# Order of the seven products, VectorE subtractions and split order in the second layer's pair stages

## The chip, the cores and the metric

The kernel runs on one core of a Trainium2 chip. The time is in device microseconds of that core, from runs of the whole program; a comparison uses the median of several runs. Before the change the median of three runs is 1150.7 us (1148.37 to 1151.74).

## The reference

Three parts follow one another. Only the third is touched by the change, beside the loads that lead to it.

```python
# 1. retention: 4 x 8 heads, 768 steps of 64 x 64 state
state = gamma * state + k[t] (x) v[t];  y[t] = q[t] @ state / 8
x = y.transpose(0, 2, 1, 3).reshape(3072, 512)
# 2. first layer: w_in 512 x 2048, w_out 2048 x 512
h = x @ w_in;  g = (a0 + a1*h + a2*h^2 + a3*h^3) / (1 + |b0||h| + |b1|h^2 + 1e-6);  x = g @ w_out
# 3. second layer, same sizes
h = x @ w_in;  g = h * clip(h + 3, 0, 6) / 6;  out = g @ w_out
```

All tensors are float32. The kernel multiplies in TensorE's reduced float32 form and keeps the accuracy by splitting each operand into a high and a low part and adding three products: high x high, high x low, low x high.

## The kernel before

The 3072 tokens are six blocks of 512. Retention and the first layer go block by block, then the second layer does blocks 0 and 1 in the plain way, in steps numbered `n` (`N1` = 96 is the first step of the second layer, `N2` = 128 the first behind its plain part). The other four blocks go as two pairs, p = 1 and 2 (`second_layer`, L1069). A pair of blocks is a 2 x 2 block matrix product, done by Strassen and Winograd's scheme with seven products in place of eight. Products are called 1 to 7 by their number `q`.

A pair has two stages. In the first, `unit(p, u, part)` (L890) forms, for each of eight slices u of the hidden dimension, the seven products of the inputs `xs[p, q]` with the weights that `win_load` fetched, in the order 1, 6, 2, 7, 5, 4 and, in the next unit, 3. VectorE joins them, and `gate` leaves the gate values of the four blocks, tiles g11, g12, g21 and g22 (`groom`). `whole_sum` makes the sums S of g21 and g22.

The second stage (L1095 to L1110) multiplies the gates with w_out. Its 14 halves are (q, k): `ORDER` gives the order of the products, k the half of the tokens. In the loop over the halves stand, for half i: the load of the next product's weights (`wout_load`, four tiles wo, on SP's queue, at k = 0), the half's 48 matmuls (`product`, L1002, 128 x 256 each), the evacuation of half i - 1 (`evac`), the split of half i + 2 (`g_split`), and for pair 1 the jobs of `xc_jobs` for pair 2's inputs.

`g_split` (L964) makes the high and low parts, tiles s, of one half in four quarters j. `source` gives what is split: for products 1, 2, 4 and 5 a gate tile or S as it stands; for 6, 7 and 3 VectorE first forms it in place (S - g11, then g11 - g21, then g12 - S). ScalarE copies the high part (L972), VectorE subtracts it (L977, by the helper line L731). In products 6, 7 and 3 the quarter j = 0 goes another way:

```python
if j == 0 and q in (6, 7, 3):
    nc.scalar.activation(lo, f32(hi), AF.Copy, scale=-1.0)              # L974
    nc.gpsimd.dma_start(out=f32(lo), in_=src, accum_op=ALU.add)         # L975, POOL's queue
```

`evac` (L1027) scales the results. Products 1 and 2 add up in bank A, 6 and 7 in bank B, 5 and 3 in bank C, and 4 starts afresh in bank B. For product 1 and 2 ScalarE does it (L1032, L1048); for 6, 3 and 4 VectorE does one operation, for 7 two (L1025). Results go out by `store` (L1019) on SP's queue.

Pair 2's inputs are loaded, combined and split by `xc_jobs(2)` (L1112), which says behind which half of pair 1 each job is emitted: `xc_load` at 5 and 6, `xc_sums` at 8 and 9, and the 14 calls of `xc_split`, three a half, from 9 on. `xc_split` is a ScalarE copy (L829) and a VectorE subtraction. Behind half 12 the first weights of pair 2 are loaded (`win_load`, L843, on SP's queue). For pair 1 the same calls are put into steps by L1304 to L1309.

Buffers of 128 x 1024 are rooms of one pool: `take` hands out the room that was given back first, `give` puts it at the end of the list. Who writes into a room waits for its last reader. Each engine and each queue works its instructions in the order of emission; every wait is a wait of all that stands behind it there.

Weight sums: the scheme needs sums of weight blocks. `prep_at(n, kind, u)` (L792) puts one into the steps: load at n - 1, four VectorE operations at n (`prep_sums`), ScalarE copies at n + 1, two VectorE subtractions at n + 2 (`prep_lo`), stores to DRAM on POOL's queue at n + 2, rooms back at n + 4. `LATE` holds the steps, counted from `N1`, of seven of them; the last three are of w_out (tiles zwo). From step 130 on a step of this list is emitted behind a unit of pair 1.

Of the kernel before, what the change touches and what calls it, by code (L numbers as in the profile page):

```python
# [12 lines left out]
AF = mybir.ActivationFunctionType  # L13
ALU = mybir.AluOpType
# [10 lines left out]
SPARE = ("wi14", "wi15", "wo14", "wo15")  # L25
WARM, WARM_AGAIN = 3, 3
PREP, FAR, AHEAD = 50, 9, 4
KEPT, LATE = 14, (18, 20, 22, 24, 31, 33, 34)
Q_CONST = 1.0 + 1e-6
LN_SCALE = 2.0**16  # L30
G_SCALE = -1.0 / LN_SCALE**2
# [3 lines left out]
def tile_retention_moe_moe2(  # L35
# [13 lines left out]
    nc = tc.nc  # L49
# [632 lines left out]


    PAIRS, FIRST = NBLK // 2, 1
    ORDER = (1, 5, 6, 7, 3, 2, 4)
    LEFT = {1: 0, 2: 1, 4: 3, 5: 4, 6: 5, 7: 6, 3: 7}
    RIGHT = {1: 0, 2: 2, 3: 3, 5: 4, 6: 5, 7: 6, 4: 7}
    smalls, bigs, spare_half, taken = deque(), deque(), ([], []), {}
# [25 lines left out]
    def take_two(name):  # L714
        return take_big(name) if bigs else (take(name + "h"), take(name + "l"))

    def give(*tiles):
        for t in tiles:
            place = taken.pop(id(t))
            if isinstance(place, tuple):  # L720
                smalls.append(place)
            else:
                place[1] -= 1
                if place[1] == 0:
                    bigs.append(place[0])

    def f32(t):
        return t.bitcast(F32)

    def tensor(engine, out, a, b, op):  # L730
        engine.tensor_tensor(out=out, in0=a, in1=b, op=op)  # L731
# [91 lines left out]
    def xc_split(p, c, q):  # L823
        a, b, d, e = (f32(t) for t in xraw[p, c])
        src = {1: a[:, 0:512], 2: b[:, 0:512], 3: b[:, 512:1024], 5: d[:, 0:512], 6: d[:, 512:1024], 7: e[:, 0:512], 4: e[:, 512:1024]}[q]
        if c == 0:
            xs[p, q] = take_two(f"x{p}_{q}")
        hi, lo = (t[:, c * 512 : (c + 1) * 512] for t in xs[p, q])
        nc.scalar.activation(hi, src, AF.Copy)  # L829
        tensor(nc.vector, lo, src, f32(hi), ALU.subtract)  # L830
        if q == 4:
            give(*xraw.pop((p, c)))


# [55 lines left out]
    def unit(p, u, part):  # L890
        nm = f"{p}_{u}"
        if part == 0:
            if u == 0:
                live[p] = ps_at.tile([128, 1024], F32, tag="at", name=f"a{p}")
            now = live[p, u] = {"A": live[p][:, 0:512]}
            mm1(p, u, 1, now["A"], True)
            if u:
                last_two(p, u - 1, 0)
            now["s1"] = g_p.tile([128, 512], F32, tag="gh", name="s1" + nm)
            nc.scalar.activation(now["s1"], now["A"], AF.Copy)  # L900
            now["B"] = ps_h.tile([128, 512], F32, tag="h", name="hB" + nm)
            mm1(p, u, 6, now["B"], True)
            now["U2"] = t2.tile([128, 512], F32, tag="u", name="U2" + nm)
            tensor(nc.vector, now["U2"], now["B"], now["s1"], ALU.add)
        elif part == 1:
            now = live[p, u]
            if u:
                mm1(p, u - 1, 3, live[p, u - 1]["C"], False)
                last_two(p, u - 1, 1)
            mm1(p, u, 2, now["A"], False)  # L910
            gate(p, 11, u, now["A"], relu(now["A"], "11_" + nm))
        else:
            now = live[p, u]
            mm1(p, u, 7, now["B"], False)
            U3 = t2.tile([128, 512], F32, tag="p", name="U3" + nm)
            tensor(nc.vector, U3, now["B"], now.pop("s1"), ALU.add)
            now["C"] = ps_h.tile([128, 512], F32, tag="h", name="hC" + nm)
            mm1(p, u, 5, now["C"], True)
            h22 = g_p.tile([128, 512], F32, tag="gl", name="h22" + nm)
            tensor(nc.vector, h22, now["C"], U3, ALU.add)  # L920
            gate(p, 22, u, h22, relu(h22, "22_" + nm))
            if (p, u) == (FIRST, 0):
                now["D"] = live[p][:, 512:1024]
            else:
                now["D"] = ps_acc.tile([128, 512], F32, tag="acc0", name="hD" + nm)
            mm1(p, u, 4, now["D"], True)
            tensor(nc.vector, U3, now["D"], U3, ALU.add)
            now["h21"] = U3

    sums, splits, wout, halves = {}, {}, {}, [(q, k) for q in ORDER for k in range(2)]

# [30 lines left out]
    def g_split(p, q, k, js=range(4)):  # L964
        if (p, q, k) not in splits:
            splits[p, q, k] = [take(f"s{p}_{q}_{k}_{i}") for i in range(4)]
        rooms = splits[p, q, k]
        for j, src in [(j, source(p, q, k, j)) for j in js]:
            hi, lo = (
                rooms[i + j // 2].rearrange("p (f t) -> p f t", f=4)[:, j % 2 * 2 : j % 2 * 2 + 2, :] for i in (0, 2)  # L970
            )
            nc.scalar.activation(hi, src, AF.Copy)  # L972
            if j == 0 and q in (6, 7, 3):
                nc.scalar.activation(lo, f32(hi), AF.Copy, scale=-1.0)  # L974
                nc.gpsimd.dma_start(out=f32(lo), in_=src, accum_op=ALU.add)  # L975
            else:
                tensor(nc.vector, lo, src, f32(hi), ALU.subtract)  # L977
        if k == 1 and 3 in js:
            dead = {7: (21, 11), 2: (12,), 4: (22,)}.get(q, ())
            give(*(groom.pop((p, x, j)) for x in dead for j in range(4)))  # L980
            if q == 3:
                give(*(sums.pop((p, j)) for j in range(4)))
# [84 lines left out]
            smalls.extend([(raw_p, "raw")] * 2)  # L1067

    def second_layer():  # L1069
        for p in range(FIRST, PAIRS):  # L1070
            for u in range(NU):
                last = u == NU - 1
                if (p, u) != (FIRST, 0):
                    unit(p, u, 0)
                    unit(p, u, 1)
                    if u > 1 and u % 2 == 0:
                        whole_sum(p, u // 2 - 1)
                    if not last:
                        win_load(p, u + 1)
                    unit(p, u, 2)  # L1080
                    if p == FIRST:
                        for parts in (begin, middle, before, after):
                            for fn, *args in parts.get(N2 + LAG + u - 1, ()):
                                fn(*args)
                if last:
                    give(*(t for q in (1, 6, 2, 7, 5, 4) for t in xs.pop((p, q))))
                    wout_load(p, ORDER[0])
                    g_split(p, 1, 0, range(3))
            g_split(p, 1, 0, (3,))
            mm1(p, NU - 1, 3, live[p, NU - 1]["C"], False)  # L1090
            last_two(p, NU - 1, 0)
            last_two(p, NU - 1, 1)
            whole_sum(p, NU // 2 - 1)
            give(*xs.pop((p, 3)))
            jobs_x = xc_jobs(p + 1) if p + 1 < PAIRS else {}  # L1095
            g_split(p, *halves[1])
            for i, (q, k) in enumerate(halves):
                at = ORDER.index(q)
                if k == 0 and at + 1 < len(ORDER):
                    wout_load(p, ORDER[at + 1])  # L1100
                product(p, q, k)
                if i:
                    evac(p, *halves[i - 1])
                if i + 2 < len(halves):
                    g_split(p, *halves[i + 2])
                for fn, *args in jobs_x.get(i, ()):
                    fn(*args)
                if p + 1 < PAIRS and (q, k) == (ORDER[-1], 0):
                    win_load(p + 1, 0)
            evac(p, *halves[-1])  # L1110

    def xc_jobs(p):  # L1112
        js = {5: [(xc_load, p, 0)], 6: [(xc_load, p, 1)]}
        splits_due = []
        for c in range(2):
            js[8 + c] = [(xc_sums, p, c, 0, nc.vector), (xc_sums, p, c, 1, nc.vector)]
            splits_due += [(xc_split, p, c, q) for q in (1, 2, 3, 5, 6, 7, 4)]
        for i, job in enumerate(splits_due):
            js.setdefault(9 + i // 3, []).append(job)
        return js  # L1120

    segs = [(0, 0, 0, CUT1), (0, 1, 0, FT), (0, 0, CUT1, FT)] + [(0, b, 0, FT) for b in range(2, NBLK)]
# [121 lines left out]
    def put(where, n, fn, *args):  # L1244
        where.setdefault(n, []).append((fn, *args))
# [41 lines left out]
    for key in (VIA, NBLK, NBLK + 1):  # L1287
        n = at_of[0, key, 0] if key < NBLK else at_of[1, key - NBLK, 0]
        for c in range(KD):

            if key == VIA:
                at, lag = n - 9 + c + 2 * (c > 1), 1
            elif key == NBLK + 1:
                at, lag = n - 5 + c, 1
            else:
                at, lag = n - 12 + 2 * c, 2
# [7 lines left out]
    for c, at in enumerate((23, 26)):  # L1304
        put(begin, N1 + at, xc_load, FIRST, c)
        put(before, N1 + at + 1, xc_sums, FIRST, c, 0, nc.vector)
        put(before, N1 + at + 2, xc_sums, FIRST, c, 1, nc.vector)
        for i, q in enumerate((1, 2, 3, 5, 6, 7, 4)):
            put(before, N1 + at + 2 + i // 2, xc_split, FIRST, c, q)  # L1309
    put(before, N2 - 3, win_load, FIRST, 0)  # L1310
    put(before, N2 - 1, win_load, FIRST, 1)
# [235 lines left out]
```

## Time and profile before

| | |
|---|---|
| median of three runs | 1150.7 us |
| profiled execution | 1151.67 us |
| its span, first to last instruction | 1149.9 us |
| mean granted TensorE clock | 0.989 |
| TensorE matmuls busy | 1108.5 us, 96% |
| VectorE busy | 926.5 us, 81% |
| ScalarE busy | 704.7 us, 61% |
| GpSimd busy | 115.7 us, 10% |

The profile is of one execution. PE is TensorE's matmuls, PEld its weight loads, DVE VectorE, ACT ScalarE, POOL GpSimd, and SPq the queue from which SyncE issues DMAs. A matmul's duration includes its way through the pipeline, so matmuls in a row overlap: the start of the next piece says more than the length of this one. Wait lists put a wait down to what came last.

In this execution pair 1's first stage begins near 802 us, its second stage runs from 887 to 977 us, pair 2's first stage from 977 to 1055 us, and its second stage from 1055 to 1146 us.

### The profile page before, as it was taken

To read this page: it belongs to the slowest core of one execution; us is meant where nothing else is said; L and a number is where in the kernel's file an instruction comes from. 1 tells how busy PE (TensorE), PEld (TensorE's weight loads), DVE (VectorE), ACT (ScalarE), POOL (GpSimd) and SP (SyncE) were. 2 spreads that over 40 slices of the span, in tenths; PEclk is the share of its full clock that TensorE was granted. 3 is DMA by queue.
4 is the path that set the end of the run, shared out by engine and by line. 5 is a ranking of instruction groups with operands and counts; after the bars stand their busy time and mean duration, and the time that the engine had idled before them with its cause. 6 is when DMAs were issued, how large, how long until landed. Compare 5 with 4: busy or idle time off the path is not lost. (4 is left out here: it accounts for less than half of the span.)

```text
span 1149.9 us, 19408 instructions
## 1 busy us (share of the span) xinstructions
PE 1108.5 (96%) x7276; PEld 927.9 (81%) x7276; DVE 926.5 (81%) x1516; ACT 704.7 (61%) x1234; POOL 115.7 (10%) x151
## 2 busy tenths in 40 slices
PE   8798999999999999999999999999999989999988
PEld 5566788888888888888888888888788889788988
DVE  5898898989998988989899788975677867567762
ACT  3898888866666667667888665544233543234451
POOL 0121101000000000000121234430010110000110
PEclk9899999999999999999999999999999999999999
DMA  9898644412113212121565969987576685944673
GB/s 334 244 234 240 181 123 95 156 47 83 48 47 103 72 47 83 47 84 37 174 182 149 347 240 401 351 292 254 197 275 232 183 253 182 389 166 146 175 209 112
DMA packets 95918, 207.41 MB, mean 180 GB/s; under 512 B 9424, under 2 KB 35152, under 8 KB 95824
## 3 DMA queue, kind: packets, MB, share of 16 engines
q1 hardware_dynamic: 75488, 156.10, 40.4%
q0 software_dynamic: 18320, 46.41, 14.4%
q10 hardware_dynamic: 2016, 3.67, 0.9%
q8 instruction: 57, 0.93, 0.3%
q14 instruction: 37, 0.30, 0.1%
HBM read 140.34 MB, written 52.95 MB: 168 GB/s over the span
## 5 line engine op out<-in xcount | busy, mean ns | idle before, releaser
L545 PE MATMUL h<-xh,wi 128*128 128x512 f32 x1024 | 279.7, 395 | 0.9 <-ACT xh L509 0.9
L545 PEld LDWEIGHTS h<-xh,wi 128*128 128x128 f32 x1024 | 189.7, 188 | 42.4 <-issue 1.3
L565 PE MATMUL acc<-gh,wo 128*128 128x512 f32 x768 | 196.0, 393 | 7.8 <-ACT gh L643 7.7
L565 PEld LDWEIGHTS acc<-gh,wo 128*128 128x128 f32 x768 | 144.0, 189 | 41.6 <-ACT gh L643 11.8
L545 PE MATMUL h<-xl,wi 128*128 128x512 f32 x512 | 138.0, 392 | 0.0
L545 PEld LDWEIGHTS h<-xl,wi 128*128 128x128 f32 x512 | 96.7, 189 | 21.0
L630 ACT ACTIVATE r<-u,cst 128x512 f32<-128x512 f32 x96 | 69.5, 724 | 65.2 <-DVE u L622 65.2
L565 PE MATMUL acc<-gl,wo 128*128 128x512 f32 x384 | 106.6, 391 | 0.3 <-DVE gl L649 0.3
L643 ACT ACTIVATE gh<-p 128x512 fp32r<-128x512 f32 x96 | 60.9, 634 | 46.7 <-DVE p L638 46.6
L565 PEld LDWEIGHTS acc<-gl,wo 128*128 128x128 f32 x384 | 72.4, 189 | 16.4 <-DVE gl L649 1.1
L1002 PE MATMUL mB<-wo,s 128*128 128x256 f32 x576 | 75.3, 295 | 8.7 <-DMA s<-S 5.2
L1002 PEld LDWEIGHTS mB<-wo,s 128*128 128x128 f32 x576 | 74.1, 203 | 9.5 <-DMA s<-S 5.7
L565 PE MATMUL acc<-wo,gh 128*128 128x512 f32 x256 | 78.8, 389 | 0.0
L613 ACT ACTIVATE p<-h,ab 128x512 f32<-128x512 f32 x96 | 73.6, 767 | 5.6 <-PE h L545 3.8
L636 DVE SCALAR_TENSOR_TENSOR u<-u,r 128x512 f32<-128x512 f32 x96 | 65.8, 686 | 12.5 <-ACT r L631 12.5
L622 DVE SCALAR_TENSOR_TENSOR u<-s,babs,u 128x512 f32<-128x512 f32 x96 | 71.5, 745 | 0.0
L637 DVE SCALAR_TENSOR_TENSOR p<-p,ab,r 128x512 f32<-128x512 f32 x96 | 71.5, 745 | 0.0
L625 DVE SCALAR_TENSOR_TENSOR p<-p,ab,h 128x512 f32<-128x512 f32 x96 | 71.1, 741 | 0.0
L621 DVE TENSOR_TENSOR p<-p,h 128x512 f32<-128x512 f32 x96 | 65.3, 680 | 7.2 <-ACT u L615 7.0
L649 DVE TENSOR_TENSOR gl<-p,gh 128x512 fp32r<-128x512 f32 x96 | 65.7, 684 | 4.3 <-ACT gh L643 4.2
L638 DVE SCALAR_TENSOR_TENSOR p<-u,p 128x512 f32<-128x512 f32 x96 | 66.4, 692 | 3.3
L615 ACT ACTIVATE u<-h,ab 128x512 f32<-128x512 f32 x96 | 66.0, 687 | 0.0
(206 smaller groups left out, 1935.2 us busy)
## 6 DMA issues: line engine op xcount, KB each, us to landing
wo<-wout SPq DMA_DIRECT2D x56, 512.0 KB, 6.1
rwi<-in_moe_w_in_dram SPq DMA_DIRECT2D x32, 512.0 KB, 5.3
rwo<-in_moe_w_out_dram SPq DMA_DIRECT2D x32, 512.0 KB, 5.5
wih<-win SPq DMA_DIRECT2D x32, 512.0 KB, 6.3
wil<-win SPq DMA_DIRECT2D x32, 512.0 KB, 6.8
T<-in_qk_t_dram SPq DMA_DIRECT2D x48, 256.0 KB, 4.3
kv<-in_kv_dram SPq DMA_DIRECT2D x32, 256.0 KB, 3.8
win<-wi POOLq DMA_DIRECT2D x16, 512.0 KB, 6.2
```

The costliest lines, as they stand in the source:

```text
L545: nc.tensor.matmul(ps, lhsT=w[:, cs], rhs=x[:, c, :], start=n == 0, stop=n == 3 * KD - 1)
L565: nc.tensor.matmul(acc[layer, blk][j], lhsT=l, rhs=r, start=f == f0 and i == 0, stop=f == f1 and i == 2)
L613: nc.scalar.activation(p, h, AF.Identity, scale=ab[:, 3:4], bias=ab[:, 2:3])
L615: nc.scalar.activation(u, h, AF.Abs, scale=ab[:, 4:5])
L622: nc.vector.scalar_tensor_tensor(out=u, in0=s, scalar=babs[:, 1:2], in1=u, op0=ALU.mult, op1=ALU.add)
L625: nc.vector.scalar_tensor_tensor(out=p, in0=p, scalar=ab[:, 1:2], in1=h, op0=ALU.add, op1=ALU.mult)
L630: nc.scalar.activation(r, u, AF.Ln, scale=1.0 / LN_SCALE, bias=ln_bias)
L636: nc.vector.scalar_tensor_tensor(out=u, in0=u, scalar=Q_CONST, in1=r, op0=ALU.add, op1=ALU.mult)
L637: nc.vector.scalar_tensor_tensor(out=p, in0=p, scalar=ab[:, 0:1], in1=r, op0=ALU.add, op1=ALU.mult)
L638: nc.vector.scalar_tensor_tensor(out=p, in0=u, scalar=-2.0 * LN_SCALE, in1=p, op0=ALU.add, op1=ALU.mult)
L649: nc.vector.tensor_tensor(out=gl, in0=tm.pop(key), in1=gh.bitcast(F32), op=ALU.subtract)
L1002: nc.tensor.matmul(out, lhsT=l, rhs=r, start=q in (1, 4, 5, 6) and t == 0 and f == 0 and i == 0, stop=f == NU - 1 and i == 2, skip_group_c ...
```

## The change

`LATE`'s last three steps become 30, 34 and 35. `ORDER` becomes 1, 5, 6, 2, 7, 4, 3, and with it the places where dead rooms are given back. All quarters of all halves are subtracted on VectorE; the negated copy and the accumulating DMA are gone. The splits of pair 2's inputs are emitted behind halves 12 (products 1, 6, 2) and 13 (7, 5, 4), and those of product 3 behind the second part of pair 2's unit 0; the four rooms of the raw inputs are given back with product 3 in place of 4. Pair 1's inputs are split in the order 1, 6, 2, 7, 5, 4, 3, in the same steps.

```diff
@@ -25,7 +25,7 @@
 SPARE = ("wi14", "wi15", "wo14", "wo15")
 WARM, WARM_AGAIN = 3, 3
 PREP, FAR, AHEAD = 50, 9, 4
-KEPT, LATE = 14, (18, 20, 22, 24, 31, 33, 34)
+KEPT, LATE = 14, (18, 20, 22, 24, 30, 34, 35)
 Q_CONST = 1.0 + 1e-6
 LN_SCALE = 2.0**16
 G_SCALE = -1.0 / LN_SCALE**2
@@ -682,7 +682,7 @@
 
 
     PAIRS, FIRST = NBLK // 2, 1
-    ORDER = (1, 5, 6, 7, 3, 2, 4)
+    ORDER = (1, 5, 6, 2, 7, 4, 3)
     LEFT = {1: 0, 2: 1, 4: 3, 5: 4, 6: 5, 7: 6, 3: 7}
     RIGHT = {1: 0, 2: 2, 3: 3, 5: 4, 6: 5, 7: 6, 4: 7}
     smalls, bigs, spare_half, taken = deque(), deque(), ([], []), {}
@@ -828,7 +828,7 @@
         hi, lo = (t[:, c * 512 : (c + 1) * 512] for t in xs[p, q])
         nc.scalar.activation(hi, src, AF.Copy)
         tensor(nc.vector, lo, src, f32(hi), ALU.subtract)
-        if q == 4:
+        if q == 3:
             give(*xraw.pop((p, c)))
 
 
@@ -970,13 +970,9 @@
                 rooms[i + j // 2].rearrange("p (f t) -> p f t", f=4)[:, j % 2 * 2 : j % 2 * 2 + 2, :] for i in (0, 2)
             )
             nc.scalar.activation(hi, src, AF.Copy)
-            if j == 0 and q in (6, 7, 3):
-                nc.scalar.activation(lo, f32(hi), AF.Copy, scale=-1.0)
-                nc.gpsimd.dma_start(out=f32(lo), in_=src, accum_op=ALU.add)
-            else:
-                tensor(nc.vector, lo, src, f32(hi), ALU.subtract)
+            tensor(nc.vector, lo, src, f32(hi), ALU.subtract)
         if k == 1 and 3 in js:
-            dead = {7: (21, 11), 2: (12,), 4: (22,)}.get(q, ())
+            dead = {7: (21, 11), 3: (12,), 4: (22,)}.get(q, ())
             give(*(groom.pop((p, x, j)) for x in dead for j in range(4)))
             if q == 3:
                 give(*(sums.pop((p, j)) for j in range(4)))
@@ -1067,12 +1063,15 @@
             smalls.extend([(raw_p, "raw")] * 2)
 
     def second_layer():
+        jobs_x = {}
         for p in range(FIRST, PAIRS):
             for u in range(NU):
                 last = u == NU - 1
                 if (p, u) != (FIRST, 0):
                     unit(p, u, 0)
                     unit(p, u, 1)
+                    for fn, *args in jobs_x.pop(14, ()):
+                        fn(*args)
                     if u > 1 and u % 2 == 0:
                         whole_sum(p, u // 2 - 1)
                     if not last:
@@ -1110,13 +1109,12 @@
             evac(p, *halves[-1])
 
     def xc_jobs(p):
-        js = {5: [(xc_load, p, 0)], 6: [(xc_load, p, 1)]}
-        splits_due = []
+        js = {}
         for c in range(2):
-            js[8 + c] = [(xc_sums, p, c, 0, nc.vector), (xc_sums, p, c, 1, nc.vector)]
-            splits_due += [(xc_split, p, c, q) for q in (1, 2, 3, 5, 6, 7, 4)]
-        for i, job in enumerate(splits_due):
-            js.setdefault(9 + i // 3, []).append(job)
+            js[5 + c] = [(xc_load, p, c)]
+            js[8 + c] = [(xc_sums, p, c, i, nc.vector) for i in range(2)]
+        for at, qs in ((12, (1, 6, 2)), (13, (7, 5, 4)), (14, (3,))):
+            js[at] = [(xc_split, p, c, q) for q in qs for c in range(2)]
         return js
 
     segs = [(0, 0, 0, CUT1), (0, 1, 0, FT), (0, 0, CUT1, FT)] + [(0, b, 0, FT) for b in range(2, NBLK)]
@@ -1305,7 +1303,7 @@
         put(begin, N1 + at, xc_load, FIRST, c)
         put(before, N1 + at + 1, xc_sums, FIRST, c, 0, nc.vector)
         put(before, N1 + at + 2, xc_sums, FIRST, c, 1, nc.vector)
-        for i, q in enumerate((1, 2, 3, 5, 6, 7, 4)):
+        for i, q in enumerate((1, 6, 2, 7, 5, 4, 3)):
             put(before, N1 + at + 2 + i // 2, xc_split, FIRST, c, q)
     put(before, N2 - 3, win_load, FIRST, 0)
     put(before, N2 - 1, win_load, FIRST, 1)
```

## Rows read from the trace of the kernel before

**Rows 1.** The page, busy time, share of the span and instructions of TensorE.

```profile
PE 1108.5 (96%) x7276; PEld 927.9 (81%) x7276; DVE 926.5 (81%) x1516; ACT 704.7 (61%) x1234; POOL 115.7 (10%) x151
```

**Rows 2.** Waits of TensorE, 885 to 985 us: total, times, longest.

```profile
PE mB L1002 <- DMA s<-S: 2.9, 1, 2.9
PE mC L1002 <- DMA s<-S: 2.1, 2, 1.3
```

**Rows 3.** The same list, 1050 to 1150 us.

```profile
PE mB L1002 <- DMA s<-g: 2.9, 1, 2.9
PE mB L1002 <- DMA s<-S: 2.4, 1, 2.4
```

**Rows 4.** Timeline of TensorE, 880 to 985 us: start, length, instructions.

```profile
899.88 11.68 PE L1002 MATMUL mC<-wo,s 128*128 128x256 f32 x96
...
965.53 11.68 PE L1002 MATMUL mB<-wo,s 128*128 128x256 f32 x96
977.05 1.10 PE L850 MATMUL a<-x,wih 128*128 128x512 f32 x4
...
981.25 1.08 PE L850 MATMUL a<-x,wih 128*128 128x512 f32 x4
...
982.62 0.62 PE L850 MATMUL hB<-x_7h,wih 128*128 128x512 f32 x2
```

**Rows 5.** Timeline of TensorE, 1040 to 1150 us.

```profile
1067.70 11.68 PE L1002 MATMUL mC<-wo,s 128*128 128x256 f32 x96
...
1087.77 13.27 PE L1002 MATMUL mB<-wo,s 128*128 128x256 f32 x96 [2.39 <-DMA s<-S]
...
1134.12 11.68 PE L1002 MATMUL mB<-wo,s 128*128 128x256 f32 x96
```

**Rows 6.** Stages by window: busy of each engine, granted clock (PEclk), DMA share, GB/s.

```profile
1085.00:1090.00 5.00, 2.61 (x15) 2.41 (x14) 4.53 (x8) 1.48 (x3) 1.19 (x1) 0.81 0.70 120
```

**Rows 7.** Tile s, 900 to 985; POOL timeline; groups by line, 700 to 1150.

```profile
DMA to landing us min/median/max: 4.5/8.1/9.4
...
1079.45 1.20 POOL L975 DMA_DIRECT2D s<-S  x1 [4.51 <-ACT s L974]
...
L974 ACT ACTIVATE s<-s 128x512 fp32r<-128x512 f32 x12 | 7.6, 633 | 10.1 <-PE mB L1002 6.7 <-PE mC L1002 3.1
```

**Rows 8.** Timeline of VectorE, 1050 to 1150 us.

```profile
1079.71 1.90 DVE L731 TENSOR_TENSOR s<-S,s 128x512 fp32r<-128x512 f32 x3 [1.41 <-ACT s L972]
1081.52 2.49 DVE L731 TENSOR_TENSOR g<-g,g 128x512 f32<-128x512 f32 x4
...
1111.28 0.69 DVE L1025 SCALAR_TENSOR_TENSOR e<-mB,e 128x512 f32<-128x512 f32 x1 [3.32 <-PE mB L1002]
...
1112.61 2.48 DVE L731 TENSOR_TENSOR s<-g,s 128x512 fp32r<-128x512 f32 x4
```

**Rows 9.** Tile wo, 880 to 985 us: its DMAs from issue to landing.

```profile
DMA to landing us min/median/max: 3.9/6.4/10.5
```

**Rows 10.** Near 970 us: ScalarE, SP's queue, chain that ended last.

```profile
969.79 0.58 ACT L1048 ACTIVATE o<-mA 128x512 f32<-128x512 f32 x1
...
970.86 0.42 SPq L843 DMA_DIRECT2D wih<-win  x1
...
972.28 8.35 DMA wil<-win
```

**Rows 11.** Timeline of all engines, 798 to 832 us.

```profile
808.14 0.69 DVE L731 TENSOR_TENSOR U<-hB,s 128x512 f32<-128x512 f32 x1 [7.15 <-ACT s L900]
...
811.78 1.62 DVE L731 TENSOR_TENSOR zwo<-zwo 128x512 f32<-128x512 f32 x3
...
813.44 1.09 DVE L731 TENSOR_TENSOR zwo<-zwo,zwo 128x256 f32<-128x256 f32 x3
...
818.07 1.19 PE L850 MATMUL a<-x,wih 128*128 128x512 f32 x4 [1.46 <-DVE U L731]
```

**Rows 12.** Timeline of POOL, 770 to 890 us.

```profile
850.69 2.14 POOL L742 DMA_DIRECT2D wout<-zwo  x3 [6.76 <-DVE zwo L731]
```

## The prediction

> **What bounds the kernel now.** The page's busy shares come first: TensorE is busy in 96% of the span [rows 1]. That average hides where the other 4% lie, so the second view is TensorE's list of waits, cut by stage. In the second stages of the two pairs nearly all that it waits for is a DMA that writes a tile s: 2.9 and 2.1 us in pair 1 [rows 2], 2.9 and 2.4 us in pair 2 [rows 3]. Those are the accumulating DMAs of the split tiles.
>
> The third view is TensorE's timeline of these stages. One second stage is 14 halves (seven products, two halves each, 48 matmuls a half). Undisturbed, two halves take 11.52 us: in pair 1 the last 96 matmuls start at 965.53 and the next stage at 977.05 [rows 4]; 5.76 us a half. From the third half on, pair 1 runs from 899.88 to 977.05, 77.17 us for 12 halves that need 69.12: **8.05 us lost** [rows 4]. Pair 2 runs from 1067.70 to 1134.12 + 11.52 = 1145.64, 77.94 us: **8.82 us lost** [rows 5]. This is more than the waits add up to (5.0 and 5.3 us), because the granted clock falls behind them: 0.81 in the 5 us around the wait that ended at 1087.77 [rows 6], a mixture of the two levels 1.2 and 2.4 GHz, and the 96 matmuls behind this wait take 13.27 instead of 11.68 us [rows 5], 1.6 us. The first two halves of each stage lose about 1 us more, while the last unit's gates drain; the change leaves those alone.
>
> **Why the DMA is late.** Of a half of products 6, 7 and 3 the first quarter goes ScalarE copy, ScalarE negated copy, issue on POOL, accumulating DMA; the other three quarters are subtracted on VectorE. The DMA of the second half of product 6 in pair 2 is issued at 1079.45 [rows 7]. Its VectorE subtractions run from 1079.71 for 1.90 us, thus to 1081.6 [rows 8]; the half is due at 1067.70 + 3 x 5.76 = 1084.98, and TensorE starts it at 1087.77 [rows 5]. The DMA alone makes it late. From issue to landing these DMAs take 4.5 to 9.4 us, median 8.1 [rows 7]. The Trainium skill says otherwise: by the fit in its page "DMA: Bandwidth & Descriptors", section "Anatomy of one DMA — SWDGE (gpsimd) path", a DMA from this queue takes 2.0 us plus its bytes by 436 GB/s, 2.6 us for these 256 KB. By that, this DMA would have landed at 1082.1 and the edit would gain nothing here; the row decides, and the sum below does not use the fit.
>
> **Edit 1: all subtractions on VectorE.** It removes 12 DMAs, 12 negated copies on ScalarE (0.63 us each [rows 7]) and adds 12 subtractions on VectorE. Four subtractions in a row take 2.48 us, 0.62 each [rows 8]; so 3.7 us more of VectorE per pair. Whether that is hidden depends on how VectorE's work is spread, which is edit 2.
>
> **Edit 2: the order 1, 5, 6, 2, 7, 4, 3.** Products 6, 7 and 3 have to form their sources first (four more VectorE operations, 2.49 us [rows 8]), so one of their halves costs 8 operations, 5.0 us, and of products 1, 5, 2, 4 four, 2.5 us. In the old order 6, 7, 3 stand together: six halves of 5.0 us and the evacuations (one operation for 6, two for 7, one for 3; 0.69 us each alone [rows 8]) come close to 5.76 us without a break. In the new order 2 stands between 6 and 7, and 4 between 7 and 3. VectorE's sum over pair 1's last 12 halves: 48 subtractions, 24 sources, 10 evacuations, and for pair 2's inputs 8 sums and 12 splits, 102 operations; at 0.62 that is 63.2 of 69.1 us, 5.9 us to spare. In pair 2 it is 82 operations, 50.8 us.
>
> A split is issued two halves ahead. Its rooms are mostly those of the product just finished, so its last subtractions can end some 1.8 us after that product (the two copies onto rooms still being read, 1.15 us, and a subtraction); it is due one half, 5.76 us, after it. That leaves about 4 us. I went through VectorE's queue in pair 1 in order, with Tn the start of half n (h0 to h13): h9 (7) is split at T8 + 1.8; then h10 (4) and four input sums to T9 + 0.9; evacuation of h8, h11 and four sums to T10 + 1.2; evacuation of h9, h12 (3) to T11 + 1.6; evacuation of h10, h13 (3) to T12 + 1.2. Each is ready 4.0 us or more before its half starts. What is queued behind these waits on VectorE are the evacuations; the product that needs one soonest is 4, which starts afresh in 7's bank: h10 at T10 needs the evacuation of h8, done at T9 + 2.2. So I cost edits 1 and 2 at nothing new, and all of 8.05 + 8.82 = **16.87 us** goes, with the clock's share. If the cover went, it would cost between 0 and what the rows show for a late half now, 0.5 to 2.9 us of wait and 1.6 us of clock. Below nothing is excluded: a half cannot be shorter than its matmuls.
>
> Rooms: 7's dead gates (8 rooms) come free two halves later than before, 3's sums and gate 12 last. At its fullest, when pair 2's second inputs are loaded (sixth index), 40 rooms (16 gates, 4 sums, 8 of weights, 8 of splits, 4 of inputs) of about 44 are held, so transfers get rooms freed by the half just ended. The weights of 7, 4 and 3 then start at T6, T8, T10 and are due two halves, 11.5 us, later; a weight load lands in 3.9 to 10.5 us, median 6.4 [rows 9], and TensorE waits for none of them now [rows 2, 3]. Nothing is added there, with little to spare at the row's maximum.
>
> **Edit 3: the inputs of pair 2.** The splits move from halves 9 to 13 to halves 12, 13 and behind unit 0's second part, in the order in which units use them. What this touches is SP's queue: the loads of pair 2's first weights stand behind the store of the half before. Now that store waits for ScalarE's output copy of product 2 at 969.79, held up by input splits and a late product 4 split, so the loads are issued at 970.86 to 972.28, and the last lands 8.35 us later, at 980.63 [rows 10]. The first twelve matmuls of pair 2 take from 977.05 to 981.25, where six take 1.37 us undisturbed (981.25 to 982.62): 4.20 against 2.74, **1.46 us lost** [rows 4]. In the new order the store before these loads waits for a VectorE evacuation at T12 + 1.9 at the latest; with the same 10.2 us from first issue to last landing the loads are there at T12 + 12.5, and the matmuls that need the last of them start at T14 + 1.37 = T12 + 12.9. I take the whole 1.46 us; if the store comes 1 us later, 0.6 of it stays. Input splits 1, 6, 2 are done at T12 + 5.6, the next six at T13 + 4.4, ahead of T14; the last two (1.3 us of VectorE in unit 0) are due 10.9 us into the stage and are covered by TensorE's matmuls of that unit. Rooms of the raw inputs are held one half longer; that is in the count above.
>
> **Edit 4: the last weight sums at 30, 34, 35 instead of 31, 33, 34.** At the step where pair 1's first unit begins, VectorE now runs six operations on zwo from 811.78 to 814.53 ahead of U, h and gate, and TensorE then waits 1.46 us for the last U [rows 11]. With sum 33 and the low part of 31 gone from this step, U can start at 811.8, 2.7 us earlier, and U's last use ends before 818.07 - 1.46 = 816.61, when TensorE comes free: **1.46 us** gained. The moved work falls into a step with VectorE idle 7.15 us [rows 11] and into the next units. The last store moves one unit (9.5 us) from 850.69 [rows 12] to 860; its readers, product 5's weights, are due at 899.88. The reordered first-pair splits come in the same steps as before: 0.
>
> **The sum.** 8.05 + 8.82 + 1.46 + 1.46 = 19.8 us. The profiled execution took 1151.67 us (span 1149.9 and 1.8 around it): 1131.9. It is 1.0 above the median of the three runs, 1150.7; against that, 1130.9. I predict **1131**.
>
> **Rivals.**
> 1. *VectorE becomes the bound in pair 1.* If its operations stood 0.69 us apart, as single ones last [rows 8], the 102 would take 70.4 us, 1.3 more than the halves; product 3's splits would be late by about that, with 1.6 us of clock, and the store before pair 2's weights would be as late as now (1.46 kept). 19.8 - 4.4 = 15.4: 1135.3. For it speaks that ScalarE copies alternate with the subtractions; against it, that rows of four take 2.48 us. The Trainium skill ("VectorE: DVE Perf Modes", "The DRAIN you can't avoid") has an operation wait until the one before has left the pipe, though not where nothing holds it; rows of four at 0.62 show the second case. Chance 0.15.
> 2. *The DMA was only the last of several late things*: ScalarE or rooms come right behind it and half of the 16.9 us stays. 1139.4. For it: VectorE itself waited 1.41 us for ScalarE ahead of the subtractions at 1079.71 [rows 8]. Against it: these were still done 3.4 us before the half was due. Chance 0.08.
> 3. *Slower: weight loads late.* Rooms come free later, so each of six loads per pair has 11.5 us. If loads took 13.5 us, each would cost 2 us of wait and 1.6 of clock, 12 times 3.6 = 43 us, net +23: 1174. It decides from 11.5 us; slower than before from about 11.6 (0.1 and 1.6, twelve times, against 19.8). The longest single load is 10.5 us [rows 9], and without twelve DMAs the engines carry less. Chance 0.03.
> 4. *It doesn't do what it says*: the new order merely moves the waits to products 7 and 3, with the clock's fall; 1150. Chance 0.03.
>
> **How the numbers follow.** The forecast, with its smaller variants (one wait of up to 3 us left over), has 0.71. What a measurement of this kernel can tell from no change is 0.3%, 3.45 us. Faster by more: the forecast, 1 and 2, 0.94; same 0.03; slower 0.03. The range goes from 1128 (the fastest run of before, 1148.37, less 19.8) to 1139.5 (rival 2).
>
> **What would show it.** In the profile after: no DMA into s; the waits of TensorE on s in both stages under 1 us together; from the third half on about 69 us in each stage; clock 1.00 throughout them; pair 2's first twelve matmuls in 2.8 us; no wait of TensorE for U near 818. VectorE busiest from product 7 on in pair 1. Wrong, if TensorE waits there for VectorE's s or for wo.

## The result, and the profile after

The changed kernel takes **1130.61 us** (median of 4 runs, 1129.61 to 1132.53); the kernel before takes 1150.75 us (4 runs, 1148.37 to 1151.74). The ratio is 0.9824, 95% interval 0.9805 to 0.9842: faster by 20.1 us. Forecast were 1131 us and 19.8 us, with a range from 1128 to 1139.5. Five more runs of the changed kernel on another chip gave 1129.54 us, ratio 0.9809 (0.9788 to 0.9830), 22.8 us under the 1152.3 of the kernel before there.

The profiled execution took 1132.53 us, span 1130.8. TensorE's list of waits from 700 us to the end, all that is left of it (line numbers are 4 lower in this kernel):

```profile
PE mA L998 <- DVE s L731: 0.8, 2, 0.4
PE a L850 <- ACT s L900: 0.5, 1, 0.5
PE mA L998 <- issue: 0.5, 2, 0.3
```

No DMA is in it, neither into s [rows 2, 3] nor of pair 2's first weights, and the wait of 1.46 us for U [rows 11] is gone. The timeline of TensorE in pair 1's second stage and the start of pair 2 (start, length, instructions):

```profile
898.78 11.68 PE L998 MATMUL mC<-wo,s 128*128 128x256 f32 x96
910.30 11.68 PE L998 MATMUL mB<-wo,s 128*128 128x256 f32 x96
921.82 11.68 PE L998 MATMUL mA<-wo,s 128*128 128x256 f32 x96
933.34 23.20 PE L998 MATMUL mB<-wo,s 128*128 128x256 f32 x192
956.38 11.68 PE L998 MATMUL mC<-wo,s 128*128 128x256 f32 x96
967.90 1.09 PE L850 MATMUL a<-x,wih 128*128 128x512 f32 x4
...
970.65 1.07 PE L850 MATMUL a<-x,wih 128*128 128x512 f32 x4
```

From the third half to the next stage it is 967.90 - 898.78 = 69.12 us, the undisturbed time to the hundredth, against 77.17 [rows 4]: 8.05 us gained. The 192 matmuls from 933.34 are products 7 and 4 without a break between them. The first twelve matmuls of pair 2 take 2.75 us, against 4.20 [rows 4]: 1.45 gained. Pair 2's stage, same view:

```profile
1057.39 11.68 PE L998 MATMUL mC<-wo,s 128*128 128x256 f32 x96
...
1114.99 11.68 PE L998 MATMUL mC<-wo,s 128*128 128x256 f32 x96
```

1114.99 + 11.52 - 1057.39 = 69.12 us again, against 77.94 [rows 5]: 8.82 gained. The same two stretches by window, in the columns of [rows 6] (busy time and instructions of PE, PEld, VectorE, ScalarE and POOL, then the granted clock, the DMA share and GB/s):

```profile
898.78:967.90 69.12, 69.12 (x579) 69.12 (x577) 58.79 (x95) 30.57 (x55) 0.00 (x0) 1.00 0.70 238
1057.39:1126.51 69.12, 69.12 (x578) 69.07 (x576) 47.44 (x76) 25.40 (x45) 0.00 (x0) 1.00 0.51 177
```

The clock is 1.00 throughout, where it had been 0.81 behind a wait. With the wait for U, the four terms are worth 8.05 + 8.82 + 1.45 + 1.46 = 19.78 us. The profiled executions differ by 19.14. Why it is less is seen from where TensorE starts pair 1's first stage, before and after:

```profile
802.04 1.07 PE L850 MATMUL a<-x,wih 128*128 128x512 f32 x4
...
802.89 1.07 PE L850 MATMUL a<-x,wih 128*128 128x512 f32 x4
```

From there to the third half the time falls from 97.84 to 95.89 us, by 1.95 where 1.46 were forecast. But the changed kernel begins this stage 0.85 us later, and its pair 2's first stage, behind the first twelve matmuls, is 0.29 us longer: 1.95 + 8.05 + 1.45 + 8.82 - 0.85 - 0.29 = 19.13. What lies ahead of pair 1 scatters: the same changed kernel begins it at 799.73 in another profiled execution. Single microseconds can't be read from the time of the whole kernel.

### The profile page after: what moved, and what is told of

Read it like the earlier page. It is cut to its first block, busy times and chain, and to the rows that moved or that the text cites. A ratio compares the mean times of both kernels' runs of the same rounds, so it can differ in the third digit from the quotient of the medians.

```text
span 1130.8 us, 19380 instructions
## 1 busy us (share of the span) xinstructions
PE 1101.3 (97%) x7276; PEld 922.4 (82%) x7276; DVE 934.5 (83%) x1528; ACT 698.6 (62%) x1222; POOL 101.2 (9%) x139
## 4 chain that ended last, share of the span: by engine, by line
PE 73%; DVE 9%; ACT 9%; DMA 6%; issue 3%; SPq 0%; ACTq 0%; DVEq 0%; POOLq 0%
PE acc L565 22%; PE h L545 22%; PE mB L998 6%; PE mC L998 4%; PE a L850 4%; PE hB L850 4%; PE hC L850 4%; PE mA L998 3%; DMA T<-in_qk_t_dram 2%; DMA rwo<-in_moe_w_out_dram 2%; PE hD L850 2%; DVE u L636 1%; DVE p L637 1%; ACT r L630 1%; DVE p L621 1%
## 5 line engine op out<-in xcount | busy, mean ns | idle before, releaser
L998 PE MATMUL mB<-wo,s 128*128 128x256 f32 x576 | 69.8, 283 | 0.0
L998 PEld LDWEIGHTS mB<-wo,s 128*128 128x128 f32 x576 | 69.4, 192 | 0.0
```

Source lines behind the costliest of these rows:

```text
L998: nc.tensor.matmul(out, lhsT=l, rhs=r, start=q in (1, 4, 5, 6) and t == 0 and f == 0 and i == 0, stop=f == NU - 1 and i == 2, skip_group_c ...
```

## The experiments

Each ran beside the kernel before on one chip, and its ratio is to that kernel's runs. The chips are not the same for all: the kernel before has medians from 1150.75 to 1152.57 us on them, so times of different experiments are compared to no better than some 2 us. What a stage gains or loses is read from the traces.

**The DMAs in the new order.** The changed kernel with the accumulating DMA put back:

```diff
-            tensor(nc.vector, lo, src, f32(hi), ALU.subtract)
+            if j == 0 and q in (6, 7, 3):
+                nc.scalar.activation(lo, f32(hi), AF.Copy, scale=-1.0)
+                nc.gpsimd.dma_start(out=f32(lo), in_=src, accum_op=ALU.add)
+            else:
+                tensor(nc.vector, lo, src, f32(hi), ALU.subtract)
```

> The changed kernel with the first quarter of products 6, 7 and 3 split by the negated copy and the accumulating DMA again (12 DMAs); the new order, the late input splits and the new steps of the weight sums stay. Theory 1 (the DMAs are what made halves late, and the order by itself hides nothing): a half whose rooms come from the product just ended has 5.76 us for a DMA that takes 4.5 to 9.4 us to land, so waits of TensorE for a DMA into s return, two to four of 1 to 3 us in each pair, each with up to 1.6 us of clock; 8 to 18 us come back, 1139 to 1149 us. Theory 2 (the order is what gains, since products with sources no longer follow each other): no wait over 1 us on s, within 3 us of the changed kernel, 1130 to 1134 us.

Measured: 1148.7 us, ratio 0.9970 (0.9953 to 0.9988). The waits from 700 us on, and the two pieces in pair 2 that stand behind them:

```profile
PE mB L1002 <- DMA s<-S: 6.4, 2, 3.3
PE mB L1002 <- DMA s<-g: 6.0, 3, 3.1
...
1083.93 7.29 PE L1002 MATMUL mB<-wo,s 128*128 128x256 f32 x46 [3.11 <-DMA s<-S]
...
1111.79 18.57 PE L1002 MATMUL mB<-wo,s 128*128 128x256 f32 x142 [3.05 <-DMA s<-g]
```

12.4 us of waits are back, with a granted clock of 0.66 in 1083 to 1088 us and in 1111 to 1116 us. From the third half on pair 1 loses 8.65 us in this trace and pair 2 9.46, 18.1 together, where the changed kernel loses nothing. Theory 1 holds at its upper end: the order hides nothing, and 18 of the 20 us hang on the DMAs.

**The old order with VectorE's subtractions.** The changed kernel with one line undone (and the places of the dead rooms with it):

```diff
-    ORDER = (1, 5, 6, 2, 7, 4, 3)
+    ORDER = (1, 5, 6, 7, 3, 2, 4)
```

> The changed kernel with the old order 1, 5, 6, 7, 3, 2, 4 (and its places where rooms are given back); all subtractions on VectorE, the late input splits, the new steps of the weight sums. Theory 1 (VectorE has the room, whatever the order): going through its queue, six halves in a row of 8 operations at 0.62 us and one or two evacuations end 2 to 4 us after the product two halves back, ahead of their due time 5.76 us: no new wait over 1 us, 1130 to 1134 us. Theory 2 (the order spreads work that VectorE could not do in a row): TensorE waits for VectorE's s in products 7 and 3, 1 to 3 us with 1.6 us of clock in each pair, 1135 to 1142 us.

Measured: 1130.35 us, ratio 0.9808 (0.9788 to 0.9828), no wait but the three that the changed kernel has. The products that need sources now follow each other, and TensorE's row of them has no break:

```profile
907.51 23.20 PE L998 MATMUL mB<-wo,s 128*128 128x256 f32 x192
930.55 11.68 PE L998 MATMUL mC<-wo,s 128*128 128x256 f32 x96
942.07 11.68 PE L998 MATMUL mA<-wo,s 128*128 128x256 f32 x96
```

These are 6 and 7, then 3, then 2, each half in 5.76 us. VectorE's last subtractions for the second half of 7 and the second half of 3 in this kernel:

```profile
917.74 2.73 DVE L731 TENSOR_TENSOR s<-g,s 128x512 fp32r<-128x512 f32 x4
...
929.54 2.49 DVE L731 TENSOR_TENSOR s<-S,s 128x512 fp32r<-128x512 f32 x4
```

They end at 920.47 and 932.03; the halves start at 930.55 - 5.76 = 924.79 and 930.55 + 5.76 = 936.31, 4.3 us later. Theory 1 holds: six halves of eight operations in a row fit too. The new order is worth nothing that these runs can tell.

**VectorE's subtractions alone.** The kernel before with the `if` of L973 and its DMA taken out, nothing else.

> The kernel before with only the 12 DMAs and negated copies replaced by subtractions on VectorE; old order, old input splits, old steps of the weight sums. Theory 1 (the DMAs are the whole of the 16.9 us): 1150.7 - 16.9 = 1133.8, with the waits at pair 2's first weights and at 818 us (1.46 us each) as before; 1132 to 1136 us. Theory 2 (order and late splits are needed for VectorE to keep up): from product 3 on, with up to 12 operations a half in pair 1, TensorE waits for VectorE's s and pair 2's first weights come several us later; 1138 to 1146 us.

Measured: 1133.49 us, ratio 0.9837 (0.9810 to 0.9864). TensorE's start of the third half and of what follows the stage in pair 1, and its third half and last piece in pair 2:

```profile
898.10 11.68 PE L998 MATMUL mC<-wo,s 128*128 128x256 f32 x96
...
967.22 1.10 PE L850 MATMUL a<-x,wih 128*128 128x512 f32 x4
...
1057.90 11.68 PE L998 MATMUL mC<-wo,s 128*128 128x256 f32 x96
...
1115.50 11.68 PE L998 MATMUL mB<-wo,s 128*128 128x256 f32 x96
```

Both stages run in 69.12 us from the third half on. The two small losses that edits 3 and 4 aim at are still there:

```profile
PE a L850 <- DVE U L731: 1.5, 1, 1.5
...
PE hB L850 <- DMA wih<-win: 0.6, 1, 0.6
```

Theory 1 holds: edit 1 by itself brings the whole 8.05 + 8.82 = 16.87 us of these stages. That the time meets the expected 1133.8 to 0.3 us is luck: on this chip the kernel before took 1152.57 us (1148.72 to 1155.21), 19.1 more, and pair 1's first stage began at 800.06 in this trace, 2.0 us earlier than the 802.04 of the kernel before, though nothing was changed ahead of it.

**The old steps of the weight sums.** The changed kernel with the last three entries of `LATE` at 31, 33 and 34.

> The changed kernel with the last weight sums at 31, 33 and 34 again. Theory 1 (VectorE's six operations on zwo make TensorE wait for U at the first unit of pair 1): that wait of 1.2 to 1.7 us is back, 1131.5 to 1132.5 us, and the trace shows it near 818 us. Theory 2 (the new split order of pair 1's inputs removed it): no wait there, the same time as the changed kernel within 0.5 us.

Measured: 1131.63 us, ratio 0.9822 (0.9800 to 0.9844). That is 1.0 us above the changed kernel, inside the scatter of the runs, but the trace shows the wait:

```profile
PE a L850 <- DVE U L731: 1.5, 1, 1.5
```

Theory 1 holds. From the first matmul of pair 1's first stage to the third half of its second it is 97.77 us here (799.68 to 897.45), against 95.89 in the changed kernel: the steps are worth 1.9 us, a little more than the wait.

**Without the weight loads.** Why does a DMA of 256 KB take 8 us? The kernel before, DMAs and all, without the loads of six of the seven products' weights (product 1's four rooms are kept to the end for it):

```diff
     def wout_load(p, q):
+        if q != ORDER[0]:
+            wout[p, q] = wout[p, ORDER[0]]
+            return
```

> The kernel before, accumulating DMAs and old order included, but in the pairs' second stages only product 1's weights are loaded and all seven products multiply with them; so 24 weight loads in each pair are left out. Theory 1 (an accumulating DMA is slow because four weight loads issued at the same time go ahead of it or share its engines): in pair 2, where nothing else is loaded, every one lands in under 5 us, no half waits for it, and pair 2's second stage loses less than 1 us from its third half on instead of 8.8; pair 1, with its input loads, loses less than 4 instead of 8.05; 1135 to 1140 us. Theory 2 (the DMA itself takes 6 to 9 us, through its descriptors or its read and write of the same bytes): landings and waits as before, 1147 to 1152 us.

Measured: 1133.03 us, ratio 0.9841 (0.9822 to 0.9860). The landings of the six DMAs of pair 1, then of pair 2 (tile s, to be held against [rows 7]):

```profile
DMA to landing us min/median/max: 3.8/3.8/5.9
...
DMA to landing us min/median/max: 3.7/3.8/4.6
```

TensorE waits for none of them, and both stages run in 69.12 us from the third half on (900.08 to 969.20, and 1059.19 to 1116.79 + 11.52). So the DMA itself takes 3.7 to 3.8 us when little else moves; the rest of the 8 us comes from the weight loads. By the fit of the Trainium skill ("DMA: Bandwidth & Descriptors", section "Anatomy of one DMA — SWDGE (gpsimd) path") it would be 2.6 us, an estimate; no run here shows so short a landing of this transfer, and the measurement decides. Theory 1 holds, more fully than expected: pair 1's input loads alone make no half wait, and the time is 2 us under the expected range. As this kernel keeps the negated copies on ScalarE, it was not those that edit 1 had to remove.

**Which halves.** When a product's first half starts, SP issues the next product's four weight loads, and at about the same time POOL issues the DMA of the product's own second half. The first half's DMA went one half earlier. The kernel before with six of the twelve DMAs, once `if j == 0 and k == 0 and ...`, once with `k == 1`:

> The kernel before with the accumulating DMA kept only in the first halves of products 6, 7 and 3 (6 DMAs); the second halves are subtracted on VectorE. Theory 1 (only a DMA that runs beside the four weight loads is late; a first half's DMA runs ahead of them): no wait for s over 0.5 us, 1132 to 1137 us. Theory 2 (any such DMA takes longer than its 5.76 us often enough): half of the loss stays, 1139 to 1146 us.

> The kernel before with the accumulating DMA kept only in the second halves of products 6, 7 and 3 (6 DMAs); the first halves are subtracted on VectorE. Theory 1 (these are the ones beside the weight loads): waits for s of 2 to 3.5 us in products 6 and 7 of both pairs stay, with up to 1.6 us of clock each, 1143 to 1151 us. Theory 2: half of the loss stays, 1139 to 1146 us, as with the first halves.

Measured: with the first halves' DMAs 1136.05 us, ratio 0.9874 (0.9853 to 0.9896); with the second halves' 1151.89 us, ratio 0.9996 (0.9980 to 1.0013). The landings in pair 1 and pair 2 and the waits for s, first halves:

```profile
DMA to landing us min/median/max: 4.2/4.3/9.4
...
DMA to landing us min/median/max: 3.8/3.8/4.1
...
PE mC L1002 <- DMA s<-S: 1.8, 1, 1.8
```

and second halves:

```profile
DMA to landing us min/median/max: 7.6/9.3/9.6
...
DMA to landing us min/median/max: 8.4/8.7/9.1
...
PE mB L1002 <- DMA s<-S: 5.6, 2, 3.1
PE mB L1002 <- DMA s<-g: 4.4, 2, 3.2
PE mC L1002 <- DMA s<-S: 2.5, 1, 2.5
```

The same transfer takes 4 us in one half and 9 in the next. The spread stands in the kernel before too; its tile s in pair 2, the stage that [rows 7] leaves out:

```profile
DMA to landing us min/median/max: 3.8/6.7/9.3
```

Six DMAs carry nearly the whole loss: with the second halves' the two stages lose 7.50 and 7.74 us in the trace, 15.2 of 16.9, and the medians can't be told from the kernel before. With the first halves' pair 2 loses nothing and pair 1 loses 3.6 us, by one late first half of product 3; theory 1 had no wait over 0.5 us there, and this one is 1.8. SP's queue in that kernel, with that half's DMA issued on POOL at 928.36:

```profile
925.11 2.07 SPq L937 DMA_DIRECT2D wo<-wout  x4
927.28 1.88 SPq L807 DMA_DIRECT2D xa<-x  x2
929.26 1.27 SPq L807 DMA_DIRECT2D xb<-x  x2
```

Four weight loads and the second half of pair 2's inputs go out around it, and it lands 9.4 us later: it is late beside weight loads too, as theory 1 has it. My expectation for the second halves gave 1151 as its upper end, and waits in products 6 and 7 only; it was 0.9 above, and product 3 waits 2.5 us as well.

**More work for VectorE.** How near is the next bound? The changed kernel with each subtraction of 6, 7 and 3 made twice:

```diff
-            tensor(nc.vector, lo, src, f32(hi), ALU.subtract)
+            for _ in range(2 if q in (6, 7, 3) else 1):
+                tensor(nc.vector, lo, src, f32(hi), ALU.subtract)
```

> The changed kernel with every subtraction of products 6, 7 and 3 made twice: 24 more VectorE operations in each pair, 14.9 us at 0.62. Theory 1 (VectorE's queue is the next bound, with 5.9 us to spare in pair 1 and 18.3 in pair 2): pair 1 loses 5 to 11 us with the clock, in products 4 and 3 and at pair 2's first weights, pair 2 under 1 us; 1136 to 1142 us. Theory 2 (VectorE is far from being a bound, most of its queue is waiting for rooms): both pairs under 2 us, 1130 to 1133 us. Theory 3 (VectorE is just at the bound in both pairs): 1145 us or more.

Measured: 1139.78 us, ratio 0.9899 (0.9884 to 0.9913), 9.2 us above the changed kernel's median. TensorE's timeline, at product 3 of pair 1, at the start of pair 2, and the last piece of pair 2:

```profile
962.68 0.98 PE L999 MATMUL mC<-wo,s 128*128 128x256 f32 x6 [0.48 <-DVE s L731]
964.01 0.98 PE L999 MATMUL mC<-wo,s 128*128 128x256 f32 x6 [0.35 <-DVE s L731]
...
972.93 1.16 PE L850 MATMUL a<-x,wih 128*128 128x512 f32 x4 [2.65 <-DMA wih<-win]
...
1064.13 11.68 PE L999 MATMUL mC<-wo,s 128*128 128x256 f32 x96
...
1121.73 11.68 PE L999 MATMUL mC<-wo,s 128*128 128x256 f32 x96
```

Pair 2 takes 14.9 us more VectorE work and still runs in 1121.73 + 11.52 - 1064.13 = 69.12 us. Pair 1 waits for VectorE's s and then for the weights of pair 2, whose loads stand behind the store of a VectorE evacuation. Pair 1's stage, whose third half starts at 896.75, ends 972.93 - 896.75 - 69.12 = 7.1 us late, and pair 2's first twelve matmuls lose 1.5 more, 8.6 together with what the clock costs. Theory 1 holds: of 14.9 us of added work pair 1 hides about 6 and pair 2 all.

**The rest of a stage's start.** The changed kernel with the first splits earlier (its first lines; product 1's second half also goes ahead of the last gates):

```diff
+                    if last:
+                        give(*(t for q in (1, 6, 2) for t in xs.pop((p, q))))
+                        wout_load(p, ORDER[0])
+                        g_split(p, 1, 0, range(2))
                     unit(p, u, 2)
```

> The changed kernel with the first splits of a second stage earlier: half of product 1's first half ahead of the last unit's third part, and product 1's second half ahead of the last unit's gates. Theory 1 (the 1.05 us that each stage still loses in its first two halves is the wait for these splits): the waits for s and the gaps there, some 0.9 us a pair, go; 1128 to 1129.5 us. Theory 2 (VectorE's work ahead of the last unit's U3 and gates delays the last first-stage product by as much): 1130 to 1132 us.

Measured: 1129.36 us, ratio 0.9808 (0.9792 to 0.9825). As that could not be told from the changed kernel, both ran again on one chip:

> The changed kernel once more, beside the next one on the same chip: 1130 to 1132 us by every theory.

> The changed kernel with the early first splits once more, beside the changed kernel on the same chip. If the 1.0 us that the first two halves gained in each stage reaches the end: 1.0 to 1.8 us under the changed kernel, 1128.5 to 1130 us. If the later start of the last first-stage product takes it back: within 0.6 us of it.

Measured: 1129.54 us (1128.76 to 1129.66) for the changed kernel, half a us below what I had expected, and 1129.17 us (1128.23 to 1130.68) with the early splits. The first two halves do get shorter, 11.57 us for 12.58, and ScalarE's copy is waited for in front of them:

```profile
883.20 11.74 PE L998 MATMUL mA<-wo,s 128*128 128x256 f32 x96 [0.53 <-ACT s L972]
894.77 11.68 PE L998 MATMUL mC<-wo,s 128*128 128x256 f32 x96
```

But most of it is taken back ahead of them. With the early splits the last first-stage product (L850, hC) starts 0.28 us later behind the one before it, and product 1 starts 2.19 us behind that, where it is 1.77 in the changed kernel (1039.28 to 1041.47 and 1039.69 to 1041.46 in pair 2). So 0.7 of the 1.0 us goes again in each pair, the second case of the expectation. 0.4 us between the medians is no difference here: no version beats the changed kernel by more than the runs scatter.

## Why the prediction was right, point by point

**What bounds the kernel: right.** The loss behind the third half was sized from TensorE's starts against 5.76 us a half, not from the list of waits, and came out at 8.05 and 8.82 to the hundredth. The 5.0 us of waits in pair 1 leave out one line of its list, a half of product 7:

```profile
PE mB L1002 <- DMA s<-g: 0.5, 1, 0.5
```

With it the waits are 5.5 and 5.3 us. They alone would have given 10.8 us, and 6.0 us, the clock's fall and what else follows a wait, would have been missed. That the whole came out at 20.1 us for a forecast of 19.8 is luck in part: on the other chip it was 22.8, and the terms of the trace add up as shown in the section on the result.

**"The DMA alone makes it late": right that VectorE and ScalarE were not late, wrong as a price of the DMA.** The 8.1 us of [rows 7] is not what this DMA takes but what it takes beside four weight loads; alone it takes 3.8. The minimum in that row, 4.5, was a hint that I passed over, and so was pair 2, where the median is 6.7. The sum was safe, as the edit removes the DMA whatever made it slow. A sum for moving the DMA to the other half, or for issuing the weights earlier, would have gone wrong by it.

**Edit 1 at no new cost: right**, and by itself the 16.87 us.

**Edit 2, the order: the step that failed.** I wrote that whether the added subtractions are hidden depends on the order. The old order gives the same time (1130.35). My walk through VectorE's queue had the answer and I did not make it for the old order in the prediction: six halves of 5.0 us and an evacuation come close to 5.76 us, but close is enough, since each has 4 us in hand. The sum over pair 1's last 12 halves was also too high: the trace has 95 operations there in place of 102, as the splits run two halves ahead and 42 subtractions fall into this stretch, not 48. They keep VectorE busy for 58.79 us, 0.62 each as taken, which leaves 10.3 us and not 5.9. That pair 1 hid about 6 us of the doubled subtractions is therefore no confirmation of the 5.9. As to the walk itself, the timeline of VectorE and SP's queue in pair 1 after the change:

```profile
932.70 2.73 DVE L731 TENSOR_TENSOR s<-g,s 128x512 fp32r<-128x512 f32 x4 [0.62 <-ACT s L972]
...
950.60 2.49 DVE L731 TENSOR_TENSOR s<-S,s 128x512 fp32r<-128x512 f32 x4
...
956.02 2.49 DVE L731 TENSOR_TENSOR s<-S,s 128x512 fp32r<-128x512 f32 x4
958.42 0.69 DVE L1021 SCALAR_TENSOR_TENSOR e<-mB,e 128x512 f32<-128x512 f32 x1
...
959.60 0.42 SPq L843 DMA_DIRECT2D wih<-win  x1
```

With T8 = 933.34 the splits of h9, h12 and h13 end at T8 + 2.1, T11 + 2.5 and T12 + 2.1, where I had 1.8, 1.6 and 1.2: the list was 0.3 to 0.9 us short and the margins of 3 to 4 us took it.

**Edit 3: right in what goes, 1.45 of 1.46 us, with some luck.** The loads are issued from 959.60, T12 + 3.2 instead of the T12 + 2.3 that I took. By my own rule some 0.5 us of wait should have stayed. None did: all four were there by 967.90 + 1.37, at most 9.7 us after the first issue. The 10.2 us that I took was a misreading: from 970.86 to 980.63 [rows 10] is 9.8. That the old order with late splits gains the same shows that it is the late splits that bring it, as it says, not the order. They are not the only way: without the weight loads these twelve matmuls take 2.75 us (969.20 to 971.95) with the old splits too.

**Edit 4: right.** With the old steps the 1.5 us wait returns. The term was a little small: the trace has 1.9 us. In the medians it is 1.0 us, which the scatter of the runs would not have shown by itself.

**The rivals.** VectorE as the bound: no; with 14.9 us more of work it is, in pair 1 alone. Late weight loads: none was waited for. Several late things behind the DMA: none, each half starts as its forerunner ends.

## What to carry to other kernels

Size a stage's loss from the starts of the bound engine against its undisturbed pace; a list of waits leaves out the clock that falls behind them. When a small transfer is late, look at the spread of its landing times before calling the median its price: here 4 us in one half and 9 in the next meant neighbours. Moving one of the two might then do as well as removing it; no run tried that. Before crediting a reordering, walk the queue in the old order too.

## What the runs showed of the hardware that I had not expected

An accumulating DMA of 256 KB inside the chip's buffers, issued from POOL, landed in 3.7 to 4.6 us in pair 2 without the weight loads, and in 7.6 to 9.6 us when four loads of 512 KB were issued around it. More than half of its time came from what was in flight beside it. Which of them the transfer engines serve first, the runs don't show.
